# A two-layer transformer kernel: LayerNorm and attention outputs transposed by DMA instead of TensorE, a six-slot score ring, and three shared PSUM banks

## The chip, the cores and the metric

The kernel runs on one core of a Trainium2 chip. The time is the device time of the program in microseconds (us), and of each kernel the median of its runs is given with the lowest and the highest. TensorE's granted clock is given as a mean; the clock records of these traces hold only full and half, so a mean of 0.942 over 736.1 us means 2 x 0.058 x 736.1 = 85 us at half clock.

## The reference

Two identical layers of windowed attention and a gated feed-forward block, on 2048 tokens of width 512, in bf16. There are 32 heads of width 16; a query sees itself and the 255 keys before it.

```python
def attention(x, wqkv, wo):               # H = 32, Dh = 16, W = 256
    q, k, v = split_heads(x @ wqkv)
    scores = einsum("bhqd,bhkd->bhqk", q, k) * Dh ** -0.5
    mask = (i - j >= 0) & (i - j < W)
    p = softmax(where(mask, scores, -1e9))
    return merge_heads(p @ v) @ wo

def glu(x, w_gate, w_up, w_down):         # F = 1792
    return (sigmoid(x @ w_gate) * (x @ w_up)) @ w_down

for _ in range(2):
    x = x + attention(layernorm(x), wqkv, wo)
    x = x + glu(layernorm(x), w_gate, w_up, w_down)
```

## The kernel before

All matmuls of the whole program are handed out over 256 "slots". A slot is one group of score matmuls (eight slots for each of the 16 key blocks of a layer) with one exp on ScalarE behind it; the rest of TensorE's work, in units of four or so matmuls, is put between the score groups as far as a budget of 2.05 us allows. TensorE executes this list strictly in order.

The eight banks of PSUM, the memory into which the matmuls of this kernel write, are given to four pools. Four banks hold the scores, one the attention sums, two everything dense (projections, gate, up, down), and one is left to the transposes (only those of the first four LayerNorm tiles take a dense bank):

```python
self.ps_s = pool("ps_s", 1, True)      # one tile of 4 banks
self.ps_o = pool("ps_o", 1, True)
self.ps_d = pool("ps_d", 2, True)
self.ps_m = pool("ps_m", 1, True)
```

There are three kinds of transposes, all on TensorE, and each is copied or read out of PSUM by VectorE. First, the normalized tokens, before the projections and the feed-forward:

```python
def ln_transpose(self, key, t, bank=None):
    ...
    pt = (bank or self.ps_m).tile([P, KT, P], BF16, name="ln_tp", tag="d" if bank else "m")
    for c in range(KT):
        nc.tensor.transpose(pt[:, c, :], xn[:, c * P:(c + 1) * P], self.ident[:])
    nc.vector.tensor_copy(out=self.xnT[key][:, :, tt * P:(tt + 1) * P], in_=pt[:])
```

Then the attention sums, where a slot later the normalized outputs `On` are transposed back for the output projection:

```python
def norm1(self, L, t, half, st, OTs):
    ...
    tps = self.ps_m.tile([P, 4, P], BF16, name="tps", tag="m")
    for c in range(4):
        nc.tensor.transpose(tps[:, c, :], OTs[:, c, :], self.ident[:])
    ...    # VectorE: Rt = 1 / row sums, On = tps * Rt
    self.at(1, 2 * T_TR, lambda: self.norm2(L, t, half, st, On))

def norm2(self, L, t, half, st, On):
    ...
    tps2 = self.ps_m.tile([P, 2, P], BF16, name="tps2", tag="m")
    ...    # ov = On, its columns in one row
    for c in range(2):
        nc.tensor.transpose(tps2[:, c, :], ov[:, c * P:(c + 1) * P], self.ident[:])
    OnT = self.ontp.tile([P, 2, P], BF16, name="OnT")
    nc.vector.tensor_copy(out=OnT[:], in_=tps2[:])
    ...    # the output projection a slot after the second half
```

The exp writes into a ring of seven slots per head whose stride lets one score matmul cover all three query blocks (384 columns), so a group is four matmuls on four row tiles. The gate and up weights are streamed from memory in 128-column chunks by the same in-order queue (SyncE's) that loads and stores everything else.

The softmax here doesn't subtract the row's maximum and nothing guards it: scores larger than these inputs give would overflow.

Of the kernel before, what the change touches and what calls it, by code (L numbers as in the profile page):

```python
# [23 lines left out]
RING_SLOTS = 7  # L24
_RING_PS = [(0, 1), (3, 1), (0, 3)]
# [7 lines left out]
T_SLOT = 2050  # L33


def ring_ps(j):
    return _RING_PS[j % 3]


def ring_slot(j, b):  # L40
    p, s = ring_ps(j)
    return p + b * s


class Net:
# [3 lines left out]
    def __init__(self, ctx, tc, A_x, wqkv, wo, w_gate, w_up, w_down, out):  # L49
# [11 lines left out]
        self.ln_st = pool("ln_st", 4)  # L61
        self.ln_xn = pool("ln_xn", 4)
        self.xnp = pool("xn_t", 3)
        self.ktp = pool("kt_tmp", 1)
# [4 lines left out]
        self.ps_s = pool("ps_s", 1, True)  # L69
        self.ps_o = pool("ps_o", 1, True)  # L70
        self.ps_d = pool("ps_d", 2, True)
        self.ps_m = pool("ps_m", 1, True)
# [9 lines left out]
        self.ring = big.tile([P, H, RING_SLOTS, P], BF16, name="PTring")  # L82

# [4 lines left out]
        for i in range(3):  # L88
            nc.sync.dma_start(out=self.wq[:, :, i * D:(i + 1) * D], in_=wq_src[:, :, i * D:(i + 1) * D])
        for tg in range(1, NTG):  # L90
            nc.sync.dma_start(out=self.xsb[:, tg * NBG:(tg + 1) * NBG, :], in_=x_src[:, tg * NBG:(tg + 1) * NBG, :])
        nc.sync.dma_start(out=self.wot[:], in_=wo.rearrange("(k p) m -> p k m", p=P))
        nc.sync.dma_start(out=self.wd[:], in_=w_down.rearrange("(c p) m -> p c m", p=P))

        self.ident = big.tile([P, P], BF16, name="ident")
# [3 lines left out]
        self.nhalf = big.tile([P, 1], F32, name="nhalf")  # L99
        nc.gpsimd.memset(self.nhalf[:], -0.5)  # L100
        self.rms = [big.tile([P, 1], F32, name=f"rm{e}") for e in range(2)]
        nc.vector.memset(self.rms[0][:], 0.0)
        for m in range(4):
# [3 lines left out]
        self.maskq = big.tile([P, 4, P], BF16, name="maskq")  # L107
        nc.gpsimd.memset(self.maskq[:], 1.0)
        nc.gpsimd.affine_select(out=self.maskq[:], in_=self.maskq[:], compare_op=ALU.is_ge, fill=0.0,
                                base=0, pattern=[[0, 4], [1, P]], channel_multiplier=-1)  # L110
        for i in range(3):
            nc.gpsimd.memset(self.Vaug[i][:], 0.0)
            onesv = self.Vaug[i][:, :, 0:VS * H].rearrange("p t (h c) -> p t h c", c=VS)[:, :, :, 16:17]
            nc.gpsimd.memset(onesv, 1.0)

        self.ready = set()
        self.due = []
        self.xn = {}
# [3 lines left out]
        self.chunk_next = 0  # L122



    def ln_stats(self, key, t):
        nc = self.nc
        st = self.ln_st.tile([P, nc.vector.BN_STATS_DIM], F32, name="ln_stats")
        mv = self.ln_st.tile([P, nc.vector.BN_AGGR_DIM], F32, name="ln_mv")
        rs = self.ln_st.tile([P, 2], F32, name="ln_rs")  # L130
        nc.vector.bn_stats(out=st[:], in_=self.xsb[:, t, :])  # L131
        nc.vector.bn_aggr(out=mv[:], in_=st[:])  # L132
        nc.gpsimd.tensor_scalar(out=rs[:, 0:1], in0=mv[:, 1:2], scalar1=1e-5, scalar2=None, op0=ALU.add)  # L133
        nc.gpsimd.tensor_tensor(out=rs[:, 1:2], in0=rs[:, 0:1], in1=self.nhalf[:], op=ALU.pow)  # L134
        self.mv[key, t] = (mv, rs)
# [9 lines left out]
    def ln_later(self, key, t, first=0):  # L145

        if first:
            self.at(first, 0, lambda: self.ln_stats(key, t))
        else:
            self.ln_stats(key, t)  # L150
        self.at(first + 1, 0, lambda: self.ln_apply(key, t))
        self.at(first + 2, KT * T_TR, lambda: self.ln_transpose(key, t))

    def ln_transpose(self, key, t, bank=None):
        nc = self.nc
        tt = t % NBG
        if tt == 0:
            self.xnT[key] = self.xnp.tile([P, KT, TGW], BF16, name="xnT")
        xn = self.xn.pop((key, t))
        pt = (bank or self.ps_m).tile([P, KT, P], BF16, name="ln_tp", tag="d" if bank else "m")  # L160
        for c in range(KT):
            nc.tensor.transpose(pt[:, c, :], xn[:, c * P:(c + 1) * P], self.ident[:])  # L162
        nc.vector.tensor_copy(out=self.xnT[key][:, :, tt * P:(tt + 1) * P], in_=pt[:])  # L163
        if tt == NBG - 1:
            self.ready.add(key)
# [3 lines left out]
    def proj_units(self, L, tg):  # L169
        key = ("p", L, tg)  # L170
        b = (L * NTG + tg) % 3
        units = []
        for which in (1, 0):
            for cq in range(NCQ):
                units.append((KT * T_MM, lambda which=which, cq=cq: self._qk(key, tg, b, which, cq)))
        for tt in range(NBG):
            units.append((KT * T_MM, lambda tt=tt: self._v(key, tg, b, tt)))
        return units

    def _qk(self, key, tg, b, which, cq):  # L180
# [10 lines left out]
        if cq == 0:  # L191
            self.kt = self.ktp.tile([P, NCQ, TGW], BF16, name="kt")
        nc.scalar.copy(out=self.kt[:, cq, :], in_=pt[:])  # L193
        for e in range(2):
            nc.vector.tensor_scalar(out=self.kTp[b][:, cq, e, :], in0=self.kt[:, cq, :],
# [14 lines left out]
    def glu_units(self, L, tg):  # L210
        key = ("g", L, tg)
        units = []
        for fc in range(FC):
            units.append((KT * T_MM, lambda fc=fc: self._gate(key, L, tg, fc)))
            units.append((KT * T_MM, lambda fc=fc: self._up(key, L, tg, fc)))
        cuts = [0, 5, 10, FC]
        for tt in range(NBG):
            for a, b in zip(cuts, cuts[1:]):
                units.append(((b - a) * T_MM, lambda tt=tt, a=a, b=b: self._down(L, tg, tt, a, b)))
        return units  # L220

    def load_chunk(self):
        i = self.chunk_next
        if i >= NGI * FC:
            return
        self.chunk_next += 1
        fc = i % FC
        w = self.wgup.tile([P, KT, 2, P], BF16, name="wgu")
        self.nc.sync.dma_start(out=w[:, :, 0, :], in_=self.wg_src[:, :, fc * P:(fc + 1) * P])
        self.nc.sync.dma_start(out=w[:, :, 1, :], in_=self.wu_src[:, :, fc * P:(fc + 1) * P])  # L230
        self.chunk_w[i] = w

    def _gate(self, key, L, tg, fc):
        nc = self.nc
        i = (L * NTG + tg) * FC + fc
        while self.chunk_next <= min(i + 2, NGI * FC - 1):
            self.load_chunk()
        w = self.chunk_w[i]
        xnT = self.xnT[key]
        ps = self.ps_d.tile([P, TGW], F32, name="gps", tag="d")  # L240
        for kt in range(KT):
            nc.tensor.matmul(ps[:], lhsT=w[:, kt, 0, :], rhs=xnT[:, kt, :], start=(kt == 0), stop=(kt == KT - 1))  # L242
        self.th = self.sigp.tile([P, TGW], BF16, name="gth")
        nc.scalar.activation(out=self.th[:], in_=ps[:], func=AF.Tanh, scale=0.5)  # L244

    def _up(self, key, L, tg, fc):
        nc = self.nc
        w = self.chunk_w.pop((L * NTG + tg) * FC + fc)
        xnT = self.xnT[key]
        ps = self.ps_d.tile([P, TGW], F32, name="ups", tag="d")  # L250
        for kt in range(KT):
            nc.tensor.matmul(ps[:], lhsT=w[:, kt, 1, :], rhs=xnT[:, kt, :], start=(kt == 0), stop=(kt == KT - 1))  # L252
        nc.vector.scalar_tensor_tensor(out=self.hT[:, fc, :], in0=self.th[:], scalar=1.0, in1=ps[:],  # L253
                                       op0=ALU.add, op1=ALU.mult)
        if fc == FC - 1:
            del self.xnT[key]

    def _down(self, L, tg, tt, a, b):
        nc = self.nc
        t = tg * NBG + tt  # L260
# [5 lines left out]
        if b == FC:  # L266
            nc.vector.tensor_tensor(out=self.xsb[:, t, :], in0=self.xsb[:, t, :], in1=self.dps[:], op=ALU.add)
            if L == 0:
                self.ln_later(("p", 1, tg), t)
# [5 lines left out]
    def scores(self, L, t, g):  # L275
# [4 lines left out]
        pj, sj = ring_ps(t)  # L280
        kTp = self.kTp[(L * NTG + t // NBG) % 3]
        ko = (t % NBG) * P
        sps = self.ps_s.tile([P, 4, 512], F32, name="Sps")
        for m in range(4):
            nc.tensor.matmul(sps[:, m, 0:N], lhsT=kTp[32 * m:32 * m + 32, cq, e, ko:ko + P],  # L285
                             rhs=self.qT[32 * m:32 * m + 32, cq, t * P:t * P + N],
                             start=True, stop=True, tile_position=(32 * m, 0))
        h0 = 8 * cq + e
        nc.scalar.activation(out=self.ring[:, h0:h0 + 7:2, pj:pj + (nb - 1) * sj + 1:sj, :],  # L289
# [3 lines left out]
    def mask(self, t, g):  # L293
        nc = self.nc
        cq, e = g // 2, g % 2
        h0 = 8 * cq + e
        r0 = self.ring[:, h0:h0 + 7:2, ring_slot(t, 0), :]
        nc.vector.tensor_tensor(out=r0, in0=r0, in1=self.maskq[:], op=ALU.mult)  # L298
        if t + 2 < NT:
            r2 = self.ring[:, h0:h0 + 7:2, ring_slot(t, 2), :]  # L300
            nc.gpsimd.affine_select(out=r2, in_=r2, compare_op=ALU.is_ge, fill=0.0, base=-1,  # L301
                                    pattern=[[0, 4], [-1, P]], channel_multiplier=1)

    def values(self, L, t, half, st):
# [15 lines left out]
        self.at(1, 4 * T_TR, lambda: self.norm1(L, t, half, st, OTs))  # L320

    def norm1(self, L, t, half, st, OTs):
        nc = self.nc
        tps = self.ps_m.tile([P, 4, P], BF16, name="tps", tag="m")
        for c in range(4):
            nc.tensor.transpose(tps[:, c, :], OTs[:, c, :], self.ident[:])  # L326
        tv = tps[:].rearrange("p c (g x) -> p c g x", x=32)
        Rt = self.otp.tile([P, 4, 4, 1], F32, name="Rt")
        nc.vector.reciprocal(out=Rt[:], in_=tv[:, :, :, 16:17])
        On = self.otp.tile([P, 4, 4, 16], BF16, name="On")  # L330
        nc.vector.tensor_tensor(out=On[:], in0=tv[:, :, :, 0:16], in1=Rt[:].to_broadcast([P, 4, 4, 16]), op=ALU.mult)
        self.at(1, 2 * T_TR, lambda: self.norm2(L, t, half, st, On))

    def norm2(self, L, t, half, st, On):
        nc = self.nc
        tps2 = self.ps_m.tile([P, 2, P], BF16, name="tps2", tag="m")
        ov = On[:].rearrange("p c g x -> p (c g x)")
# [25 lines left out]

    def run(self):
        streams = []

        def add(kind, L, tg):
            units = self.proj_units(L, tg) if kind == "p" else self.glu_units(L, tg)
            streams.append([(kind, L, tg), units, self.gi_free_slot(L * NTG + tg) if kind == "p" else 0])

# [119 lines left out]
```

## Time and profile before

| | before |
|---|---|
| time, median of 2 (lowest to highest) | 735.62 us (734.07 to 737.18) |
| span of the profiled run | 736.1 us |
| TensorE / VectorE / ScalarE busy | 85% / 62% / 62% |
| first scores, last scores start at | 30.30, 660.6 us |
| TensorE without a matmul, after the first scores | 89 us |
| mean granted clock, time at half clock | 0.942, 85 us |
| waits around the transposes | 76 us |

Read it in this order: the fullest engine (TensorE), then whether it is really computing while it is "busy" (the clock says that 85 us ran at half speed), then what it waits for when it is not. The idle time in the table is the sum of the gaps between the matmuls of the trace; the waits come from the table of TensorE's waits. The lines themselves are in the prediction below.

### The profile page before, as it was taken

What the parts mean: (1) busy time and instruction counts of PE and PEld (TensorE: products, weight loads), DVE (VectorE), ACT (ScalarE), POOL (GpSimd) and SP (SyncE); (2) the same over time, 40 slices, a digit from 0 to 9 for tenths busy, and PEclk for the clock granted to TensorE, in tenths of its full rate; (3) what the DMA queues carried; (4) which work ended last, traced back from release to release, by engine and by line L of the source; (5) the groups of instructions that cost most, each with busy time, mean ns of one, the idle gap of its engine ahead of it and who ended that gap; (6) DMA issues with size and microseconds to landing.
All of it is one profiled execution on the core that took longest, in us unless ns stands there. A gap on an engine that the chain in (4) does not pass through costs nothing.

```text
span 736.1 us, 15556 instructions
## 1 busy us (share of the span) xinstructions
PE 628.3 (85%) x6400; PEld 281.4 (38%) x6400; DVE 459.1 (62%) x1015; ACT 456.5 (62%) x465; POOL 219.5 (30%) x367
## 2 busy tenths in 40 slices
PE   1777866998788998798897899878999999999998
PEld 1233333443333444344333344333444444444443
DVE  3376765576487767667577567758577677665232
ACT  0657866676756787455866687737877677542130
POOL 6144433233343334310233333324333333000000
PEclk9959955899999999899999899979999999999999
DMA  9300000331002311022120203200132043135260
GB/s 293 78 2 1 1 2 1 71 87 45 1 2 58 87 31 29 2 58 59 42 46 2 45 8 89 64 1 2 43 89 59 31 100 88 29 81 121 72 144 29
DMA packets 126727, 38.49 MB, mean 52 GB/s; under 512 B 118720, under 2 KB 126656, under 8 KB 126656
## 3 DMA queue, kind: packets, MB, share of 16 engines
q1 hardware_dynamic: 126656, 37.50, 21.3%
q8 instruction: 50, 0.82, 0.5%
q14 instruction: 21, 0.17, 0.1%
HBM read 35.39 MB, written 2.10 MB: 51 GB/s over the span
## 4 chain that ended last, share of the span: by engine, by line
PE 63%; DVE 21%; ACT 8%; POOL 4%; issue 3%; ACTq 0%; POOLq 0%
PE ups L252 12%; PE gps L242 12%; PE dps L264 12%; ACT PTring L289 7%; PE Sps L285 7%; PE proj_ps L186 5%; DVE ln_stats L131 4%; PE OPps L350 4%; PE OTps L314 3%; DVE xn L141 3%; DVE PTring L298 3%; PE tps L326 3%; DVE xnT L163 3%; DVE xsb L352 2%; POOL ln_rs L134 2%
## 5 line engine op out<-in xcount | busy, mean ns | idle before, releaser
L289 ACT ACTIVATE PTring<-Sps 128x1536 bf16<-128x1536 f32 (+2 forms) x256 | 351.4, 1373 | 123.0 <-PE Sps L285 105.8
L301 POOL TENSOR_SCALAR_AFFINE_SELECT PTring<-PTring 128x512 bf16<-128x512 bf16 x224 | 156.6, 708 | 229.9 <-ACT PTring L289 229.9
L298 DVE TENSOR_TENSOR PTring<-PTring,maskq 128x512 bf16<-128x512 bf16 x256 | 123.0, 481 | 36.2 <-ACT PTring L289 35.8
L253 DVE SCALAR_TENSOR_TENSOR hT<-gth,ups 128x512 bf16<-128x512 bf16 x112 | 76.8, 685 | 77.7 <-PE ups L252 60.4
L244 ACT ACTIVATE gth<-gps 128x512 bf16<-128x512 f32 x112 | 66.7, 596 | 83.4 <-PE gps L242 81.0
L252 PE MATMUL ups<-xnT,wgu 128*128 128x512 bf16 x448 | 117.5, 385 | 0.5 <-DVE hT L253 0.5
L242 PE MATMUL gps<-xnT,wgu 128*128 128x512 bf16 x448 | 117.0, 384 | 0.0
L264 PE MATMUL dps<-wd,hT 128*128 128x512 bf16 x448 | 112.3, 393 | 0.0
L285 PE MATMUL Sps<-qT,kTp 32*128 32x384 bf16 (+2 forms) x1024 | 89.6, 338 | 20.7 <-ACT PTring L289 20.5
L133 POOL TENSOR_SCALAR ln_rs<-ln_mv 128x1 f32<-128x1 f32 x64 | 18.4, 287 | 218.3 <-DVE ln_mv L132 218.3
L285 PEld LDWEIGHTS <-kTp 32*128 32x128 bf16 x1024 | 30.5, 91 | 129.2 <-issue 128.9
L186 PE MATMUL proj_ps<-xnT,wq 128*128 128x512 bf16 x256 | 67.5, 402 | 3.4 <-ACT kt L193 1.9
L162 PE MATMUL ln_tp<-ident,xn 128*128 128x128 bf16 x256 | 28.7, 242 | 45.7 <-DVE xn L141 39.9
L264 PEld LDWEIGHTS <-hT 128*128 128x128 bf16 x448 | 42.3, 101 | 45.7 <-issue 5.2
L252 PEld LDWEIGHTS <-wgu 128*128 128x128 bf16 x448 | 40.5, 99 | 48.0 <-issue 9.2
L319 DVE CAST OTs<-OTps 128x512 bf16<-128x512 f32 x64 | 44.1, 689 | 23.4 <-PE OTps L314 23.2
L242 PEld LDWEIGHTS <-wgu 128*128 128x128 bf16 x448 | 41.7, 99 | 43.4 <-issue 2.5
L314 PE MATMUL OTps<-PTring,Vaug 128*32 128x128 bf16 x2880 | 54.6, 227 | 0.0
L326 PE MATMUL tps<-ident,OTs 128*128 128x128 bf16 x256 | 26.7, 231 | 26.4 <-DVE xnT L163 26.1
L314 PEld LDWEIGHTS <-Vaug 128*32 128x32 bf16 x2880 | 43.0, 100 | 11.5 <-issue 10.4
L141 DVE TENSOR_SCALAR xn<-xsb,ln_mv,ln_rs 128x512 bf16<-128x512 bf16 x64 | 38.2, 601 | 12.8 <-POOL ln_rs L134 11.3
L131 DVE BATCH_NORM_STATS2 ln_stats<-xsb 128x6 f32<-128x512 bf16 x64 | 44.2, 691 | 3.1 <-DMA xsb<-in_A_x_dram 1.5
(37 smaller groups left out, 449.1 us busy)
## 6 DMA issues: line engine op xcount, KB each, us to landing
wgu<-in_B_w_gate_dram SPq DMA_DIRECT2D x112, 128.0 KB, 2.4
wgu<-in_B_w_up_dram SPq DMA_DIRECT2D x112, 128.0 KB, 2.8
out_dram<-xsb SPq DMA_DIRECT2D x16, 128.0 KB, 1.7
wd<-in_B_w_down_dram SPq DMA_DIRECT2D x1, 1792.0 KB, 12.6
wq<-in_A_wqkv_dram SPq DMA_DIRECT2D x3, 512.0 KB, 5.6
xsb<-in_A_x_dram SPq DMA_DIRECT2D x3, 512.0 KB, 8.4
xsb<-in_A_x_dram SPq DMA_DIRECT2D x4, 128.0 KB, 2.3
wot<-in_A_wo_dram SPq DMA_DIRECT2D x1, 512.0 KB, 8.6
```

What stands on the lines that cost most here:

```text
L131: nc.vector.bn_stats(out=st[:], in_=self.xsb[:, t, :])
L186: nc.tensor.matmul(pt[:], lhsT=self.wq[:, kt, c0:c0 + P], rhs=xnT[:, kt, :], start=(kt == 0), stop=(kt == KT - 1))
L242: nc.tensor.matmul(ps[:], lhsT=w[:, kt, 0, :], rhs=xnT[:, kt, :], start=(kt == 0), stop=(kt == KT - 1))
L244: nc.scalar.activation(out=self.th[:], in_=ps[:], func=AF.Tanh, scale=0.5)
L252: nc.tensor.matmul(ps[:], lhsT=w[:, kt, 1, :], rhs=xnT[:, kt, :], start=(kt == 0), stop=(kt == KT - 1))
L253: nc.vector.scalar_tensor_tensor(out=self.hT[:, fc, :], in0=self.th[:], scalar=1.0, in1=ps[:], op0=ALU.add, op1=ALU.mult)
L264: nc.tensor.matmul(self.dps[:], lhsT=self.hT[:, fc, tt * P:(tt + 1) * P], rhs=self.wd[:, fc, :], start=(fc == 0), stop=(fc == FC - 1))
L285: nc.tensor.matmul(sps[:, m, 0:N], lhsT=kTp[32 * m:32 * m + 32, cq, e, ko:ko + P], rhs=self.qT[32 * m:32 * m + 32, cq, t * P:t * P + N], s ...
L289: nc.scalar.activation(out=self.ring[:, h0:h0 + 7:2, pj:pj + (nb - 1) * sj + 1:sj, :], in_=sps[:, :, 0:N].rearrange("p w (b c) -> p w b c" ...
L298: nc.vector.tensor_tensor(out=r0, in0=r0, in1=self.maskq[:], op=ALU.mult)
L301: nc.gpsimd.affine_select(out=r2, in_=r2, compare_op=ALU.is_ge, fill=0.0, base=-1, pattern=[[0, 4], [-1, P]], channel_multiplier=1)
L314: nc.tensor.matmul(OT[32 * g:32 * g + 32, col, :], lhsT=Va[:, jj % NBG, VS * h:VS * h + 32], rhs=self.ring[:, h, ring_slot(jj, t - jj), :] ...
```

## The change

The intent is to take work and waits off TensorE: the DMA engines transpose the LayerNorm tiles and the attention outputs, the PSUM bank that becomes free joins the dense ones, and a smaller ring makes room in SBUF. The core of the diff:

```diff
-RING_SLOTS = 7
+RING_SLOTS = 6
+RING = [(2, 3, 1), (4, 2, 0), (3, 4, 5)]
+LN_DMA = True
+ON_DMA = True
...
-        self.ps_d = pool("ps_d", 2, True)
-        self.ps_m = pool("ps_m", 1, True)
+        self.ps_d = pool("ps_d", 3, True)
...
+        if LN_DMA:
+            nc.sync.dma_start_transpose(out=dst, in_=xn[:])
+        else:
+            pt = self.ps_d.tile([P, KT, P], BF16, name="ln_tp", tag="d")
...
-        tps = self.ps_m.tile([P, 4, P], BF16, name="tps", tag="m")
+        tps = self.ps_d.tile([P, 4, P], BF16, name="tps", tag="d")
...
+        if ON_DMA:
+            OnT = self.ontp.tile([P, 2, P], BF16, name="OnT")
+            nc.sync.dma_start_transpose(out=OnT[:], in_=ov)
+            st[half] = OnT
+            if half == 1:
+                self.at(ON_LAG, KT * T_MM, lambda: self.oproj(L, t, st))
+        else:
+            self.at(1, 2 * T_TR, lambda: self.norm2(L, t, half, st, ov))
```

Three more things change with it. With six slots, the query blocks of two in three key blocks are no longer consecutive in the ring, so their score group is split into two or three rounds of narrower matmuls:

```diff
-        for m in range(4):
-            nc.tensor.matmul(sps[:, m, 0:N], ...)
+        for i, b, n in pieces:
+            for m in range(4):
+                nc.tensor.matmul(sps[:, m, i * P:(i + n) * P], ...)
```

The order of units is new: only the first key and query chunks are computed before the first scores, the first and the last four-tile GLU group are each cut into two half-wide streams, and weights come in 256-column chunks. And masks are applied to two groups at a time. Smaller changes go along: the budget of a slot is 2.00 us instead of 2.05, the value matmuls stand one slot later, and one small LayerNorm instruction moves from GpSimd to VectorE. Note that the flags keep both ways of transposing in the changed kernel.

## The prediction

> **What bounds the kernel now.** I read the page's shares first, then the table of windows, then the waits of TensorE, then a timeline of one typical stretch.
>
> ```profile
> PE 628.3 (85%) x6400; PEld 281.4 (38%) x6400; DVE 459.1 (62%) x1015; ACT 456.5 (62%) x465; POOL 219.5 (30%) x367
> ...
> PEclk9959955899999999899999899979999999999999
> ```
>
> TensorE is the fullest engine, no other is near it, and its clock was cut early on. The windows below start with the time before the first scores, then give 32 "slots" each (a slot is one group of four score matmuls, one exp and whatever is placed between them; there are 256), and last what follows the last slot. After the window come each engine's busy us, then the granted clock.
>
> ```profile
> 0.00:30.30 30.30, 15.31 (x64) 6.66 (x64) 9.14 (x30) 7.73 (x12) 12.81 (x23) 1.00 0.78 225
> 30.30:114.60 84.30, 59.33 (x579) 27.34 (x579) 58.00 (x139) 58.17 (x57) 35.58 (x61) 0.76 0.01 1
> 114.60:195.20 80.60, 67.94 (x750) 30.22 (x750) 48.18 (x107) 57.16 (x54) 26.86 (x41) 0.87 0.21 47
> ...
> 518.00:591.20 73.20, 68.40 (x785) 30.79 (x784) 48.72 (x104) 55.83 (x52) 25.74 (x41) 1.00 0.25 59
> ...
> 660.60:736.00 75.40, 71.46 (x373) 30.99 (x372) 27.44 (x45) 14.93 (x25) 0.79 (x2) 1.00 0.38 91
> ```
>
> Three losses show. TensorE idles 705.7 - (628.3 - 15.3) = 93 us after the first scores. A clock of 0.76 over 84.3 us is 40 us at half clock, 0.87 over 80.6 us is 21 us, and the later windows add some 23 us, so about 84 us run at half speed. And 75 us of matmuls come after the last scores, when ScalarE and VectorE have nothing to share. Who causes the idle time:
>
> ```profile
> PE ln_tp L162 <- DVE xn L141: 39.9, 40, 12.0
> PE tps L326 <- DVE xnT L163: 26.1, 34, 2.6
> PE Sps L285 <- ACT PTring L289: 20.5, 34, 1.8
> PE ln_tp L162 <- DVE xnT L163: 5.4, 4, 1.4
> PE tps L339 <- DVE xnT L163: 4.8, 6, 1.3
> ```
>
> The four waits around the transposes are 39.9 + 26.1 + 5.4 + 4.8 = 76.2 us, of which about 14 us lie in the start. TensorE works in order, so a LayerNorm transpose stuck behind VectorE stops all the matmuls behind it. One such slot, beginning at 549.60:
>
> ```profile
> 549.60 0.34 PE L285 MATMUL Sps<-qT,kTp 32*128 32x384 bf16 x4
> 550.22 0.40 PE L162 MATMUL ln_tp<-ident,xn 128*128 128x128 bf16 x4 [0.28 <-DVE xn L141]
> 551.48 0.38 PE L326 MATMUL tps<-ident,OTs 128*128 128x128 bf16 x4 [0.86 <-DVE xnT L163]
> 551.71 1.03 PE L242 MATMUL gps<-xnT,wgu 128*128 128x512 bf16 x4
> 552.66 0.34 PE L285 MATMUL Sps<-qT,kTp 32*128 32x384 bf16 x4
> ```
>
> TensorE waits 0.28 us for the normalized tile, then 0.86 us because the attention transpose needs the one PSUM bank that the LayerNorm transpose holds until VectorE has copied it out. The slot takes 3.06 us; its neighbours take 2.1 to 2.3 us and are dense.
>
> **What the Trainium skill says.** "VectorE: DVE Perf Modes", The three transpose paths, gives 390 ns for a 128x128 bf16 transpose on TensorE and 1309 ns through the DMA crossbar. The trace shows 219 ns as the median of one on TensorE and 56 ns from one start to the next; it has no DMA transpose. "DMA: Bandwidth & Descriptors", Latency and other measured facts, gives 261 GB/s for DMA transposes with a broken middle dimension, so 64 KB is 0.25 us and 128 KB 0.5 us, and its Anatomy section puts a fixed cost of about 2 us on a DMA; the plain 128 KB loads here land after 2.4 to 2.8 us, which agrees. "TensorE: Matmul & The Clock Gate", The HAM clock gate, says that the array falls to half clock when it has been idle and rises after sustained work; the 0.76 of the windows is that, and the matmul spacing goes from 216 to 427 ns in it. "TensorEngine Tiling (Array Packing)", Key Properties, says a change of tiling mode drains TensorE; here the first score matmul starts 312 ns after a 512-column matmul that needs 216, so 96 ns go there, and the next begins 262 ns later where 384 columns at 2.4 columns a ns need 160.
>
> **The change, part by part.** I price TensorE's own work from starts in the trace at full clock: 216 ns per 512-column matmul, 360 ns per score group (96 + 262), 13.5 ns per value matmul and 150 ns at the end of its group of 48 (0.80 us), 57 ns per transpose.
>
> Before: (448 x 3 + 256 + 128 + 128) = 1856 matmuls of 512 columns x 216 ns = 401 us; 256 score groups x 0.36 = 92; 60 value groups x 0.80 = 48; 640 transposes x 57 ns = 36. Sum 577 us. The other 159 us of 736 are waits, clock and the two ends.
>
> After, by the order in which its instructions stand:
> - The 256 LayerNorm and 128 output transposes leave TensorE: -384 x 57 ns = -22 us. The 256 in between stay.
> - The six-slot ring no longer lets every score group be one run. 1984 score matmuls stand in place of 1024: 240 extra rounds of four. They move the same columns in all; I choose 0.1 us for each extra round (a weight load lasts 91 ns in the trace): +24 us.
> - Half-width GLU streams: 448 matmuls of 256 columns for 224 of 512, 224 more issues at some 2.7 ns (216 ns less 512 columns at 2.4 a ns), +1 us.
>
> So the dense sum stays, 581 us by adding it slot by slot. What changes is the rest:
> - LayerNorm and bank waits: the 62 us after the start go, as nothing on TensorE now waits for VectorE's normalization but the reader of the finished transpose, two slots later. Three ordinary PSUM banks instead of two also take away the 148 ns that each up group waits in the dense end (28 x 0.148 = 4 us).
> - Thin slots: a slot can't be shorter than the loop exp, scores, exp, about 1.45 + 0.5 = 1.95 us (exp is 1453 ns; the scores bring the next exp 0.44 to 0.6 us after they start). In the new order 20-odd slots hold less than that (0, 2, 4, 22 to 23, 37 to 39, 53 to 57, 65 to 71), and the shortfall adds up to 26 us. Before it was 39 us.
> - Start: only the first key and query chunks come before the first scores, 8 matmuls instead of 48. The transposes queue behind 3.5 MB of loads (293 GB/s in the first slice: 12 us). I take first projections at about 14.5 us, first scores at about 20 instead of 30.
> - Clock: fewer gaps early, so I halve the penalty. 84 us at half clock and 80% busy cost 34 us; I leave 18.
> - New waits for DMA: the output projection stands two slots after the normalized output, about 4.5 us, of which some 1.5 us pass before VectorE has written it. That leaves 3 us for issue, 64 KB and landing, estimated at 2.3 to 3.5 us by the plain loads. I allow 0.5 us x 32 = 16 us. LayerNorm transposes mostly have more slack, as streams queue.
> - Other engines: VectorE loses 26.6 us and 18.3 us of copies and half of its mask instructions; GpSimd halves its too. Neither bounds, so that is worth nothing but promptness.
> - End: 43 us instead of 72 of dense work after the last scores. The dense sum already holds it: the work moved into slots that were thin.
>
> Sum: 581 + 26 thin + 14.5 start + 18 clock + 16 DMA waits + 3.5 last store + 7 for small waits = 666 us.
>
> **The rivals.** First, DMA transposes are slow or stand in line. All DMAs go through one in-order queue, where a gate and up pair of loads takes 0.9 us to issue, and a transpose waits there for VectorE with weight loads behind it. For it: nothing in the trace measures one, and the slack is about equal to the latency. Against it: two slots were chosen as the lag, and the DMA engines are only 21% busy. Landing at 5 us would make 32 waits of 2 us, plus some for LayerNorm: 720 us or more; at 8 us, 800.
>
> Second, the broken score groups cost more than they save: each extra round might drain like a mode change, 0.2 to 0.25 us, and lie on the loop to the exp too. That adds 25 to 35 us: about 695. Against it: rounds are of the same mode.
>
> Third, ScalarE becomes the bound once TensorE's waits go: 256 exps and the copies and tanhs, 456 us of busy time plus 5 us for half-width tanhs. That is far under 660, but locally (exp and two copies, 2.6 us in a projection slot) it can hold scores back: +10 us.
>
> Fourth, the half-width streams at the end must load 512 KB per pair of hidden chunks in 1.7 us of matmuls, 300 GB/s, as much as the trace has ever moved. If the loads fall behind, the end grows by 5 to 15 us.
>
> **Range and chances.** The sum is 666; better clock and no DMA waits give about 632; slow transposes or dear score rounds give 700 to 718. Same (721 to 750) needs both rivals or landings of 5 us and more; slower needs landings of about 7 us. I give 0.88 faster, 0.08 within 2%, 0.04 slower.
>
> **What would show it.** Right: waits for transposed LayerNorm tiles and for VectorE are nearly gone from TensorE's list; first scores near 20 us; last scores near 615 to 620 and 47 us behind them; the mean slot in the middle about 2.25 us; score groups with three rounds some 0.2 us longer than with one. Wrong: output projection or projections waiting on DMA by tens of us; a transpose landing after 4 us or more; PEclk under 0.8 over a third of the span; gaps of over 0.2 us inside score groups.

## The result, and the profile after

The changed kernel took 676.83 us (median of 2, 676.31 to 677.35) beside 735.62 us before: a ratio of 0.9198 with a 95% interval of 0.9162 to 0.9235. Ratios here are the mean time of one kernel's runs over that of the other's of the same rounds, so they are not quite the ratio of the medians quoted.

The shares and the clock of the changed kernel, to be laid beside those of before:

```profile
PE 592.3 (88%) x7200; PEld 282.1 (42%) x7200; DVE 422.9 (63%) x851; ACT 459.1 (68%) x493; POOL 164.9 (24%) x191
...
PEclk9899899789868999999999999999999998999889
```

TensorE is 36 us less busy, and the three slices at 5 tenths are gone. But slices at 6 to 8 tenths remain in the first third. The table of windows of the changed kernel (time from slot 0, then slots 32 to 63, 192 to 223, and what follows the start of the last scores; then each engine's busy us, the clock, the DMA share and GB/s) says where:

```profile
21.47:103.87 82.40, 65.19 (x768) 32.61 (x767) 53.24 (x119) 66.24 (x78) 24.50 (x27) 0.94 0.36 85
103.87:184.80 80.93, 65.43 (x941) 35.81 (x940) 51.85 (x105) 54.97 (x56) 21.43 (x24) 0.89 0.31 78
...
476.40:546.90 70.50, 69.03 (x863) 30.82 (x863) 43.75 (x81) 56.14 (x53) 19.54 (x20) 1.00 0.35 83
...
616.60:675.70 59.10, 48.54 (x363) 30.93 (x362) 20.89 (x46) 11.35 (x29) 0.55 (x1) 0.94 0.46 128
```

The first 64 slots are hardly shorter than before (82.4 and 80.9 us against 84.3 and 80.6). The gain was made around them: of the 60 us between the two spans, 9 lie before the first scores, 31 in slots 96 to 223, which in windows of 32 took 73.2 to 84.3 us each before and now take 70.5 to 72.6, and 16 behind the last scores. The last scores start at 616.58 instead of 660.6 us, and 59 us follow them, of which TensorE is without a matmul for 7 us. Over the whole kernel it is without one for 62 us after the first scores (89 before), and the mean clock of 0.957 makes 58 us at half speed (85 before).

What TensorE waits for now (total us, times, longest):

```profile
PE Sps L337 <- ACT PTring L341: 21.3, 29, 1.7
PE proj_ps L224 <- DMA xnT<-xn: 17.2, 1, 17.2
PE gps L284 <- DMA wgu<-in_B_w_gate_dram: 14.9, 7, 4.4
PE tps L383 <- DVE OTs L371: 7.7, 7, 1.7
PE gps L284 <- DMA xnT<-xn: 5.4, 3, 2.9
...
PE OPps L419 <- DMA OnT<-On: 1.5, 4, 0.4
```

The waits for VectorE's normalization are gone, the output projections wait 1.5 us in all, and a line is new: 14.9 us for gate weights. Before, no wait of a matmul for weights stood in the list. The loads did not become slow; they are issued late. The DMA issues (count, KB each, median us from issue to landing):

```profile
wgu<-in_B_w_gate_dram SPq DMA_DIRECT2D x70, 256.0 KB, 3.2
...
xnT<-xn SPq DMA_TRANSPOSE x64, 2.4
OnT<-On SPq DMA_TRANSPOSE x64, 2.3
```

And a stretch of the queue that issues them, with the gap on TensorE that it causes. On SyncE's queue:

```profile
85.87 0.51 SPq L273 DMA_DIRECT2D wgu<-in_B_w_up_dram  x1
91.70 1.18 SPq L397 DMA_TRANSPOSE OnT<-On  x1
92.99 0.51 SPq L272 DMA_DIRECT2D wgu<-in_B_w_gate_dram  x1
93.54 0.51 SPq L273 DMA_DIRECT2D wgu<-in_B_w_up_dram  x1
```

and on TensorE:

```profile
93.50 0.60 PE L295 MATMUL ups<-xnT,wgu 128*128 128x256 bf16 x4
96.17 0.61 PE L284 MATMUL gps<-xnT,wgu 128*128 128x256 bf16 x4 [2.07 <-DMA wgu<-in_B_w_gate_dram]
```

The queue issues nothing from 86.4 to 91.70, because at its head stands the transpose of an attention output that VectorE writes only from 91.24 to 91.67. Behind it stands a weight load that could have gone since about 88.3, when TensorE had done with the weight buffer that it fills (three are used in turn). It goes at 92.99, lands about 3.2 us later, and TensorE, which works through half-wide chunks in half the time, has by then stood still for 2.07 us. In the kernel before, this queue had been waiting for TensorE to release weight buffers (279 and 249 us in its own list of waits), so it was always ahead.

The same happens at the end: another such transpose is issued at 625.78, the loads behind it at 627.08, and a gate group that would have followed at 627.5 starts at 630.23. The outputs are not alone in this: a LayerNorm tile's transpose is issued at 637.15, the loads behind it from 638.52 on, and the gate group that starts at 641.58 has stood still for 2.60 us.

### The profile page after: what moved, and what is told of

It is laid out like the page before. It is cut to its first block, busy times and chain, and to the rows that moved or that the text cites. A ratio compares the mean times of both kernels' runs of the same rounds, so it can differ in the third digit from the quotient of the medians. Undisturbed runs are those within 1.5% of the kernel's fastest.

```text
span 675.6 us, 17143 instructions
## 1 busy us (share of the span) xinstructions
PE 592.3 (88%) x7200; PEld 282.1 (42%) x7200; DVE 422.9 (63%) x851; ACT 459.1 (68%) x493; POOL 164.9 (24%) x191
## 4 chain that ended last, share of the span: by engine, by line
PE 64%; ACT 12%; DVE 10%; DMA 9%; issue 2%; SPq 1%; POOL 1%; ACTq 0%; POOLq 0%; DVEq 0%
PE ups L295 14%; PE gps L284 13%; PE dps L307 10%; ACT PTring L341 9%; PE Sps L337 8%; PE proj_ps L224 7%; PE OTps L366 6%; PE OPps L419 3%; DMA wgu<-in_B_w_up_dram 3%; PE tps L383 2%; DVE xn L162 2%; DMA wgu<-in_B_w_gate_dram 2%; DVE ln_stats L152 2%; DVE PTring L348 2%; DMA xnT<-xn 2%
## 5 line engine op out<-in xcount | busy, mean ns | idle before, releaser
L353 POOL TENSOR_SCALAR_AFFINE_SELECT PTring<-PTring 128x1024 bf16<-128x1024 bf16 x112 | 124.4, 1113 | 182.5 <-ACT PTring L341 182.5
L284 PE MATMUL gps<-xnT,wgu 128*128 128x512 bf16 (+1 forms) x560 | 126.4, 351 | 20.7 <-DMA wgu<-in_B_w_gate_dram 14.9
L297 DVE SCALAR_TENSOR_TENSOR hT<-gth,ups 128x512 bf16<-128x512 bf16 (+1 forms) x140 | 81.0, 579 | 94.1 <-PE ups L295 71.5
L295 PE MATMUL ups<-xnT,wgu 128*128 128x512 bf16 (+1 forms) x560 | 126.5, 351 | 5.1 <-DMA wgu<-in_B_w_up_dram 1.7
L287 ACT ACTIVATE gth<-gps 128x512 bf16<-128x512 f32 (+1 forms) x140 | 71.3, 512 | 81.1 <-PE gps L284 76.2
L337 PE MATMUL Sps<-qT,kTp 32*128 32x128 bf16 (+2 forms) x1984 | 87.6, 248 | 25.6 <-ACT PTring L341 21.3
L155 POOL TENSOR_TENSOR ln_rs<-ln_rs,nhalf 128x1 f32<-128x1 f32 x64 | 38.3, 599 | 288.5 <-DVE ln_rs L154 283.6
L348 DVE TENSOR_TENSOR PTring<-PTring,maskq 128x1024 bf16<-128x1024 bf16 x128 | 98.8, 772 | 0.3 <-ACT PTring L341 0.2
L224 PE MATMUL proj_ps<-xnT,wq 128*128 128x512 bf16 x256 | 66.9, 398 | 18.2 <-DMA xnT<-xn 17.2
L284 PEld LDWEIGHTS <-wgu 128*128 128x128 bf16 x560 | 51.9, 101 | 64.3 <-DMA wgu<-in_B_w_gate_dram 17.9
L295 PEld LDWEIGHTS <-wgu 128*128 128x128 bf16 x560 | 52.7, 102 | 49.1 <-issue 8.3
L224 PEld LDWEIGHTS <-wq 128*128 128x128 bf16 x256 | 23.2, 101 | 44.9 <-DMA xnT<-xn 17.2
```

The lines of the kernel that those rows point to most:

```text
L224: nc.tensor.matmul(pt[:], lhsT=self.wq[:, kt, c0:c0 + P], rhs=xnT[:, kt, :], start=(kt == 0), stop=(kt == KT - 1))
L284: nc.tensor.matmul(ps[:, 0:w], lhsT=wt[:, kt, 0, (fc % 2) * P:(fc % 2 + 1) * P], rhs=xnT[:, kt, c0:c0 + w], start=(kt == 0), stop=(kt == K ...
L287: nc.scalar.activation(out=self.th[:, 0:w], in_=ps[:, 0:w], func=AF.Tanh, scale=0.5)
L295: nc.tensor.matmul(ps[:, 0:w], lhsT=wt[:, kt, 1, (fc % 2) * P:(fc % 2 + 1) * P], rhs=xnT[:, kt, c0:c0 + w], start=(kt == 0), stop=(kt == K ...
L297: nc.vector.scalar_tensor_tensor(out=self.hT[:, fc, 0:w], in0=self.th[:, 0:w], scalar=1.0, in1=ps[:, 0:w], op0=ALU.add, op1=ALU.mult)
L337: nc.tensor.matmul(sps[:, m, i * P:(i + n) * P], lhsT=kTp[32 * m:32 * m + 32, cq, e, ko:ko + P], rhs=self.qT[32 * m:32 * m + 32, cq, (t + ...
```

## The experiments

Twelve kernels ran; each ran four times (one with the profile and three rounds) beside the kernel before on the same chip. The first call (experiments 1 to 4) ran on another chip than the other two; the kernel before took 736.76 us in the first two calls, and 736.89 in the third. All results were correct.

### 1. Both transposes back on TensorE

```diff
-LN_DMA = True
-ON_DMA = True
+LN_DMA = False
+ON_DMA = False
```

> The changed kernel with both kinds of transposes back on TensorE, into one of the three rotating PSUM banks; ring, banks, streams and start stay new. Theory A (the DMA transposes earn their keep by taking TensorE's in-order waits away as well as its 384 x 57 ns = 22 us of issue): 22 us plus some 0.3 us of waiting for each of 64 LayerNorm transposes = about +40 us, so 710 to 725 us, close to the kernel before. Rival B (only the issue time counts, since the third bank already cures the bank wait): +22 us, about 699. Rival C (the gain came from the banks, the streams and the start; the transposes are nearly free in either place): within 8 us of the changed kernel's 676.8.

Measured: 681.53 us (680.05 to 684.31), ratio 0.9257 (0.9232 to 0.9283). Without any DMA transpose, nearly the whole gain is still there; the DMA transposes are worth 5 us of 60. First scores start at 17.15 us here, 4.3 us earlier than in the changed kernel. The clock is 0.987, so only 18 us ran at half speed against 58 us, and the wait for the normalized tile is 20.7 us instead of 39.9. At some 88% busy, 40 us less at half clock are worth about 40 x 0.5 x 0.88 = 18 us, so by this sum the clock pays for most of the 22 us of transposes that came back to TensorE.

### 2. and 3. One of the two back on TensorE

```diff
-LN_DMA = True      # run 2
+LN_DMA = False
-ON_DMA = True      # run 3
+ON_DMA = False
```

> Only the LayerNorm transposes back on TensorE. Theory A: 256 x 57 ns = 15 us of issue plus 0.3 us x 64 of waits = +34 us, about 710. Rival B: +15 us, about 692. Rival C: within 6 us of 676.8. At the start alone the TensorE path may win 5 us, since the DMA transposes there stand behind the loads.

> Only the attention-output transposes back on TensorE. Theory A: 128 x 57 ns = 7 us of issue plus up to 0.3 us x 64 of waits for VectorE, and the queue is freed of 64 transposes that hold weight loads up (about -5 us): +5 to +20 us, 682 to 697. Rival B: +7 us less the freed queue, about 680. Rival C: within 3 us.

Measured: 695.46 us (690.75 to 696.67), ratio 0.943 (0.9388 to 0.9473), with LayerNorm on TensorE; 666.63 us (664.53 to 668.18), ratio 0.9049 (0.9026 to 0.9071), with the outputs on TensorE. So the two halves of the idea have opposite signs. Taken from the version with both on TensorE, DMA for LayerNorm wins 681.5 - 666.6 = 15 us, and adding DMA for the outputs loses 10 us again. In the other order the signs are the same: the outputs by DMA lose 14 us, and LayerNorm by DMA then wins 19. In the run with only the outputs on TensorE the waits for gate and up weights are 7.0 + 3.4 us instead of 14.9 + 1.7. In all four versions, these waits add up to 4.9 us with no DMA transpose, 10.4 with LayerNorm's alone, 11.8 with the outputs' alone and 16.6 with both. With none, these are the lines:

```profile
PE ups L295 <- DMA wgu<-in_B_w_up_dram: 2.7, 5, 1.6
PE gps L284 <- DMA wgu<-in_B_w_gate_dram: 2.2, 3, 1.1
```

So both kinds hold the weights up, and about equally; LayerNorm's win on balance, as TensorE is also rid of twice as many transposes and of the wait for the normalized tile. A LayerNorm tile takes one DMA transpose of 128 KB; the outputs take two of 64 KB for each token tile, and each holds the queue 1.2 us and waits there for VectorE, as LayerNorm's do too.

### 4. Every score group in three rounds

```diff
-            if pieces and pieces[-1][1] + pieces[-1][2] == b:
+            if False:
```

> Every score group broken into single blocks of 128 columns: 2880 score matmuls in 720 rounds instead of 1984 in 496. As priced in the prediction (0.1 us a round): 224 x 0.1 = +22 us, about 699. As the trace after reads (full slots with one round and with three both last 2.11 us): within 3 us of 676.8.

Measured: 679.40 us (676.58 to 683.05), ratio 0.9227 (0.9189 to 0.9264). The extra rounds went from 240 to 464, so 224 more rounds cost 2.6 us, with ranges that overlap: about 0.01 us each (0.03 us at the far ends of both intervals), not the 0.1 us that I had charged. In the trace of the changed kernel the first matmul of a second round starts 57 ns after the start of the last one of the first round, where the matmuls of one round start 2 to 4 ns apart, and full slots with one, two and three rounds all last 2.11 us. From the first score matmul of a group to the next matmul behind it, TensorE needs 273, 276 and 279 ns (medians at full clock) with one, two and three rounds.

### 5. One bank for all transposes again, with both on TensorE

```diff
-        self.ps_d = pool("ps_d", 3, True)
+        self.ps_d = pool("ps_d", 2, True)
+        self.ps_m = pool("ps_m", 1, True)
-            pt = self.ps_d.tile([P, KT, P], BF16, name="ln_tp", tag="d")
+            pt = self.ps_m.tile([P, KT, P], BF16, name="ln_tp", tag="m")
...    (tps and tps2 likewise)
```

> On the version with all transposes on TensorE (681.5): the PSUM banks as in the kernel before, two for the dense work and one that all three kinds of transposes share. If the shared bank was the loss (waits for its copy-out were 26.1 + 5.4 + 4.8 = 36 us before, and the dense work waits 148 ns for a bank in its pairs): +25 to +45 us, 707 to 727. If the new placement of the transposes and the streams is what helps: within 10 us of 681.5.

Measured: 756.48 us (754.88 to 757.75), ratio 1.0271 (1.0232 to 1.031): slower than the kernel before, and 29 us beyond the range that I had expected. The wait that leads TensorE's list in this kernel (total us, times, longest):

```profile
PE ln_tp L179 <- DVE On L394: 57.7, 33, 2.7
```

And one slot of its timeline on TensorE, from one score group on:

```profile
563.02 0.35 PE L338 MATMUL Sps<-qT,kTp 32*128 32x128 bf16 x8
563.30 0.40 PE L384 MATMUL tps<-ident,OTs 128*128 128x128 bf16 x4
565.70 0.61 PE L179 MATMUL ln_tp<-ident,xn 128*128 128x128 bf16 x4 [2.00 <-DVE On L394]
566.10 1.91 PE L285 MATMUL gps<-xnT,wgu 128*128 128x512 bf16 x4
```

The LayerNorm transpose stands directly behind an attention transpose, both want the same bank, and VectorE must first compute the reciprocals and the products out of it. TensorE stands still for 2.00 us, and the gate matmuls behind, which need neither, stand with it. The gate group then takes 1.91 us instead of 1.03: the clock has dropped as well.

### 6. The GLU groups undivided, with both on TensorE

```diff
-("g", 0, 0, 2), ("g", 0, 2, 2), ...  ("g", 1, 12, 2), ("g", 1, 14, 2)]
+("g", 0, 0, 4), ...                  ("g", 1, 12, 4)]
```

> On the version with all transposes on TensorE: the first and the last GLU group undivided, as before the change. If the halves are what fills the thin slots: the first can begin some 14 slots later, 13 slots with 1 us of work or less, so +10 to +20 us, and the last half's work stays in the end, so about 695. If the halves cost in weight loads (14 more pairs of 512 KB) what they gain: within 6 us of 681.5, or faster.

Measured: 680.22 us (676.32 to 681.06), ratio 0.9226 (0.9185 to 0.9268), against 681.53 with the halves: no difference that these runs can show. The 4.9 us of waits for weights that the halves had even without DMA transposes, all of them after 636 us, are gone from TensorE's list here, but the clock is lower (0.972 against 0.987).

### 7. Outputs and the first four LayerNorm tiles on TensorE, weights loaded ahead

```diff
-ON_DMA = True
+ON_DMA = False
-        if LN_DMA:
+        if LN_DMA and key != ("p", 0, 0):
...
+        self.at(8, 0, lambda: [self.load_chunk() for _ in range(3)])
```

> On the version with only the output transposes on TensorE (666.6): the first four LayerNorm transposes on TensorE too, so that they don't stand behind the first loads, and the first three pairs of GLU weights loaded from slot 8 on. TensorE's first projection comes at 17.1 us there and its inputs are written by 8.9 us: about -6 us. The first GLU stream waits about 3 us for its weights and drops to half clock after: -3 to -5 us. So 655 to 659. If the time is set elsewhere: within 3 us of 666.6.

Measured: 659.21 us (657.53 to 660.67), ratio 0.8948 (0.8907 to 0.8989). Beside experiment 3 this is 7.4 us less, for two edits that were not run apart. First scores start 4 us earlier, and the waits for gate and up weights fall from 10.4 to 4.4 + 1.6 us. The start of the changed kernel shows why it was late there. On SyncE's queue:

```profile
8.08 7.04 SPq L174 DMA_TRANSPOSE xnT<-xn  x4
```

and on TensorE:

```profile
17.23 3.57 PE L224 MATMUL proj_ps<-xnT,wq 128*128 128x512 bf16 x8 [17.23 <-DMA xnT<-xn]
```

The four normalized tiles are written by 8.84 us, but their transposes are still being issued at 15.1 us, behind loads that keep the DMA engines 94% busy in this stretch.

### 8. Weight loads on GpSimd's queue

```diff
-        self.nc.sync.dma_start(out=w[:, :, 0, :], ...
+        self.nc.gpsimd.dma_start(out=w[:, :, 0, :], ...
...    (up weights likewise)
```

> The changed kernel, its GLU weight loads issued from GpSimd's queue, so that no transpose stands in front of them. If the 10 us between it (676.8) and the version with output transposes on TensorE (666.6) come from weight loads held up in the one queue: TensorE's 16.6 us of waits for weights fall to under 6 and the time to 664 to 669. If they come from the longer road of the output transposes themselves (two slots of lag before the projection): within 4 us of 676.8. GpSimd's own issue time could add some us.

Measured: 690.11 us (684.99 to 691.65), ratio 0.9359 (0.9311 to 0.9407): 13 us slower than the changed kernel. The waits for gate and up weights do fall, from 14.9 + 1.7 to 3.4 + 5.2 us. But in its profiled run, at 684.99 us the fastest of the four, GpSimd's busy time goes from 164.9 to 271.5 us, as issuing 140 loads takes it 107 us, and others now wait: TensorE 10.8 us for a dense bank that VectorE releases late, 8.8 us for LayerNorm tiles, 5.9 us for transposed outputs. This run neither proves nor refutes that the shared queue costs 10 us by itself, since it puts a new load on an engine that LayerNorm and the masks need.

### 9. The kernel before, with nothing but its banks changed

```diff
-        self.ps_d = pool("ps_d", 2, True)
-        self.ps_m = pool("ps_m", 1, True)
+        self.ps_d = pool("ps_d", 3, True)
...    (ln_tp, tps and tps2 taken from ps_d)
```

> The kernel before with nothing changed but the PSUM allocation: the two dense banks and the one bank for all transposes become three banks that everything dense and every transpose share in turn. Order of instructions, ring, streams and masks stay as before. Theory (the single transposing bank made the waits, of which the kernel before lists 26.1 + 5.4 + 4.8 = 36 us behind its copies out of that bank; the 39.9 us for the normalized tile are the order's): the waits for the bank go and those for the normalized tile stay, about 700 us, with a range of 690 to 712. Rival (the banks only matter in the new order, which puts the LayerNorm transpose right behind an attention transpose): within 2% of 736. A stricter form of the theory (the banks are the whole gain): 680 or less.

Measured: 689.53 us (686.07 to 690.88), ratio 0.9358 (0.9308 to 0.9407). These few words are worth 47 us. Two of TensorE's waits in it (total us, times, longest):

```profile
PE ln_tp L161 <- DVE xn L140: 42.6, 47, 12.0
...
PE tps L325 <- DVE xnT L162: 1.4, 2, 0.7
```

And the slot that the prediction showed for the kernel before, as its timeline on TensorE has it now:

```profile
507.21 0.34 PE L284 MATMUL Sps<-qT,kTp 32*128 32x384 bf16 x4
507.84 0.40 PE L161 MATMUL ln_tp<-ident,xn 128*128 128x128 bf16 x4 [0.28 <-DVE xn L140]
508.07 0.39 PE L325 MATMUL tps<-ident,OTs 128*128 128x128 bf16 x4
508.43 1.02 PE L241 MATMUL gps<-xnT,wgu 128*128 128x512 bf16 x4
509.38 0.34 PE L284 MATMUL Sps<-qT,kTp 32*128 32x384 bf16 x4
```

The wait of 0.28 us for the normalized tile is still there, the 0.86 us for the bank are not, and the slot takes 2.17 us instead of 3.06. Over the whole kernel the wait for the normalized tile stays (42.6 us against 39.9) and the one for the bank goes from 26.1 to 1.4 us. TensorE's idle time after the first scores falls from 89 to 59 us. The rest is the clock: 0.970, so 41 us at half speed instead of 85. At TensorE's 80% busy, 44 us less at half clock are worth about 44 x 0.5 x 0.8 = 18 us; 30 + 18 is 48, and the spans differ by 736.1 - 686.9 = 49.

### 10. DMA transposes with the old banks

```diff
-        self.ps_d = pool("ps_d", 3, True)
+        self.ps_d = pool("ps_d", 2, True)
+        self.ps_m = pool("ps_m", 1, True)
-        tps = self.ps_d.tile([P, 4, P], BF16, name="tps", tag="d")
+        tps = self.ps_m.tile([P, 4, P], BF16, name="tps", tag="m")
```

> The changed kernel, both transposes by DMA, with two dense banks and one bank left to the transposes of the attention sums in between (all that stays on TensorE). It completes the square of transposes (DMA or TensorE) and banks (old or new): TensorE with old banks 756, TensorE with new banks 682, DMA with new banks 677. If the DMA transposes are a second way around the shared bank, this stays near the changed kernel, 680 to 695 us, and my prediction's step was right under the old banks alone. If the third dense bank matters by itself, 720 us or more.

Measured: 688.17 us (685.80 to 691.13), ratio 0.9345 (0.9295 to 0.9395). With experiments 1, 5 and 9 this completes a table (medians in us):

| | one bank for transposes, two dense | three banks shared |
|---|---|---|
| old order, transposes on TensorE | 735.6 (before) | 689.5 |
| new order, transposes on TensorE | 756.5 | 681.5 |
| new order, transposes by DMA | 688.2 | 676.8 (after) |

Under the old banks, DMA transposes are worth 68 us; under the new banks, 5 us. They and the shared banks are two ways around the same obstacle, and either is nearly enough. The table also shows that the new order, taken with its ring and streams, is no gain by itself: it loses 21 us with the old banks and wins 8 with the shared ones.

### 11. Two shared banks, the eighth left empty

```diff
-        self.ps_d = pool("ps_d", 3, True)      # with both transposes on TensorE
+        self.ps_d = pool("ps_d", 2, True)
```

> All transposes on TensorE in the shared rotation, as in the run of 681.5 us, but with two banks in the rotation instead of three and the eighth bank left empty. If what hurts is one bank of its own for the transposes (a wait for the copy out of just that bank), this lies nearer to 682 than to 756: under 710. If the number of banks in the rotation is what counts, 730 us or more, since transposes and matmuls then share two.

Measured: 774.21 us (773.44 to 774.56), ratio 1.0511 (1.0475 to 1.0547). This is the slowest kernel of all, so my expectation of under 710 us was wrong. So a bank of their own is not worse for the transposes than no third bank at all (756 us against 774). But with the same three banks, sharing them instead of setting one apart is worth 75 us. What counts in these runs is that all three rotate. With two, projections, gates, ups and downs all wait for VectorE to finish the attention outputs (10.1, 8.2, 6.7 and 6.2 us); the first two of these lines:

```profile
PE proj_ps L224 <- DVE On L393: 10.1, 9, 1.5
PE gps L284 <- DVE On L393: 8.2, 10, 0.9
```

### 12. Experiment 7 with undivided GLU groups

```diff
+("g", 0, 0, 4) and ("g", 1, 12, 4) of experiment 6, on top of experiment 7
```

> The fastest run so far (659.2 us: output transposes and the first four LayerNorm transposes on TensorE, three weight chunks loaded ahead) with the first and last GLU groups undivided. With the groups divided, TensorE waited 4.4 + 1.6 us for gate and up weights, and the last two half-wide groups read the weights once more than one wide one does. If the half streams' loads still cost at the end, 650 to 656 us; if halves stay net zero as in the TensorE version (680.2 against 681.5), within 3 us of 659.

Measured: 656.99 us (655.48 to 658.07), ratio 0.892 (0.8887 to 0.8953). Beside the 0.8948 of experiment 7, this is at most a small gain: the intervals overlap. The waits for weights have shrunk to 0.7 us, but undivided groups have a price that the timeline of TensorE shows just as clearly:

```profile
608.14 1.03 PE L419 MATMUL OPps<-wot,OnT 128*128 128x512 bf16 x4
614.68 1.86 PE L284 MATMUL gps<-xnT,wgu 128*128 128x512 bf16 x4 [5.51 <-issue]
```

The last group needs all four of its tiles, and between the last output projection and the first gate there is nothing left to do for 5.5 us while the last tile is added, normalized and transposed (the DMA transpose is issued at 612.20). The half-wide streams hide that, and pay for it with weight loads. This is the fastest kernel, 20 us below the changed one. Whole first and halved last group would be the next thing to try; it did not run.

## Why the prediction was right, and where its steps were not

The time was predicted at 666 us and measured at 676.8, inside the range, with the predicted sign. The steps fare less well than the sum, and that it came so close is in part luck.

**The waits go: right. Why they go: mis-sized.** The prediction said that 62 us of LayerNorm and bank waits go because nothing on TensorE waits for the normalization any more, and gave the third bank 4 us, for the dense end. The waits did go. But the bank change alone is worth 47 us (experiment 9), and the DMA transposes only 5 us once the banks are shared (experiment 1). Had the banks stayed, the step would have held: under the old ones the DMA transposes alone take away 68 us (experiments 5 and 10). The third bank was the term mis-sized: I saw the 0.86 us that a transpose waited for the bank, and read it as a reason to move the transposes rather than to share the banks. The Trainium skill has the general advice in "Perfetto Trace Analysis", Optimizing Tensor Performance, Matmuls: independent groups should rotate through different PSUM banks, so that one is emptied while the next is filled. This agrees, and shows its size: 774, 756 and 682 us with two shared, two plus one, and three shared banks.

**Score rounds, +24 us: wrong.** They cost nothing that can be measured (experiment 4). My 0.1 us was the duration of a weight load (91 ns), as if it came on top; the second round starts 57 ns after the first, and that disappears in the slot. The rival of draining rounds, 25 to 35 us, falls with it.

**DMA waits of the output projection, 16 us: wrong place.** They came to 1.5 us, as the transposes land in 2.3 us, at the lower end of what I had taken (one of the signs of being wrong, a landing after 4 us or more, did show in 9 of the 128, the longest, of 7.5 us, in the start). Three waits for LayerNorm tiles took 5.4 us more. In place of the 16 us came 14.9 + 1.7 us for gate and up weights, which my sum did not hold at all. The fourth rival saw that wait at the end only (5 to 15 us), and for loads that fall behind the half-wide streams. That much may be right of it: without any DMA transpose 4.9 us are left, all in the end, and they go with the halves (experiment 6). The rest comes with the transposes in the queue. The first rival had the right mechanism, a transpose that waits for VectorE with weight loads behind it, and I dismissed it because the DMA engines were only 21% busy. A queue's order is not its load. That the outputs' transposes lose time and LayerNorm's win some is shown (experiments 2 and 3), and so is that either kind adds 5 to 7 us of waits for weights. That it is the queue's head that costs, and not some other effect of them, rests on the traces (each of the five longest waits for gate weights, 2.07 to 4.36 us, follows a load that was issued right behind a transpose, four times one of an output and once one of a LayerNorm tile), as experiment 8 stayed inconclusive.

**Start: right mechanism, 3 us short.** First projection at 17.23 us instead of 14.5, first scores at 21.47 instead of about 20. The transposes did queue behind the loads, for longer than I took.

**Clock: direction right, too much hoped for.** I halved the half-clock time from 84 us; it fell to 2 x 0.043 x 675.6 = 58 us. With both transposes on TensorE it fell to 18. New gaps for weights and a thinner TensorE list go together with the lower clock early on, but no run here isolates the clock from the gaps.

**Thin slots and other engines.** TensorE still waits 21.3 us for the exp, as before (20.5), and my 26 us for the thin slots is not told apart from other waits by any run. No other engine became the bound, as said: ScalarE is at 68%, VectorE at 63%.

**End: 59 us instead of 47 after the last scores.** 7 us of it is TensorE standing still, mostly for weights, and a clock of 0.94 over 59.1 us is another 7 us at half speed.

So errors cancelled. The rounds were charged at 24 us and took nothing that shows. In their place stand 62 us of idle TensorE where the sum had 49 (thin slots, DMA waits and small waits), some 7 us more of clock loss (58 x 0.5 x 0.85 = 25 against 18), 3 us of start, and a remainder. Added up again with measured terms: 581 - 24 = 557 of dense work, 17.2 of start, 62 idle, 25 for the clock and 3.3 behind the last matmuls make 665 of the 675.6 us of the profiled run; some 11 us I can't assign to a term.

## What to carry to other kernels

When an in-order engine waits for a buffer, count the buffers that rotate before moving the work away: here one bank moved from "reserved" to "shared" gave 47 us, where the whole change gave 59, without touching an instruction's engine. A transpose moved to a DMA queue still waits for its producer, and everything behind it in that queue waits too, so move those whose input is early, and keep latency-critical loads ahead of them. And when a change has several parts, build the version with only the cheapest one: it may be most of the gain.

## What the Trainium skill lacked or had wrong

- "DMA: Bandwidth & Descriptors" gives a rate for DMA transposes, but, apart from cycle counts for "previous generations" in its part on trn3, not how long one holds the queue that issues it: each took 1.18 to 1.20 us to issue (median of 64), against about 0.5 us for a plain load of 256 KB, and 64 KB and 128 KB landed after 2.3 and 2.4 us, nearly independent of size.
- No page that I found gives the cost of a transpose waiting at the head of an in-order queue: here 5.3 us without an issue (86.4 to 91.70), and 16.6 us of waits for weights with DMA transposes against 4.9 without.
- "TensorEngine Tiling (Array Packing)" says that a change of mode drains TensorE, and apart from a general overhead for each matmul gives no cost for further rounds in the same mode: 224 extra rounds moved the time by 2.6 us, within the spread.
- "TensorE: Matmul & The Clock Gate" describes the return to full clock after some 3.4 us of sustained work, but not how full that work must be: in the kernel before, the clock stayed at half from 105.6 to 130 us with TensorE busy 61 to 73% of each stretch, and rose at 135.0 after 4.5 us without a gap (130.45 to 135.0). Nor does it say how short of idle a fall can come: the clock fell at 36.0, 70.1 and 94.0 us, and TensorE had been busy 15, 25 and 42% of the 3.4 us before.
